# A planned kernel for a gated recurrence and a two-layer block: new load costs in the planner, weight reloads in fewer transfers, and another order of the last products and stores

## The chip, the cores and the metric

The kernel runs on one core of one Trainium2 chip. The metric is device time in microseconds (us), from one launch of the kernel. The kernel before was run ten times: median 593.34 us, lowest 590.56, highest 594.98. One more execution was recorded by the hardware profiler; it took 590.61 us, of which 588.9 lie between its first and last instruction. Its mean granted TensorE clock was 0.995 of full speed.

## The reference

Everything is computed in 32-bit floats. A gated recurrence comes first (batch 4, 8 heads, 768 tokens, 48 dims a head), then a block of two matrix products with `h - tanh(h)` between them:

```python
state = np.zeros((B, H, D, D), dtype=np.float32)
for t in range(S):
    state = alpha[:, :, t, :, None] * state + np.einsum('bhd,bhe->bhde', k[:, :, t], v[:, :, t])
    y[:, :, t] = np.einsum('bhd,bhde->bhe', q[:, :, t], state)

x = y.transpose(0, 2, 1, 3).reshape(B * S, H * D)     # 3072 tokens x 384
h = x @ w_in                                          # 384 x 2048
g = h - np.tanh(h)
out = g @ w_out                                       # 2048 x 384
```

The two weights reach the kernel as 64-bit words, and the kernel turns them into 32-bit floats itself.

## The kernel before

**Units.** The 3072 tokens are cut into 12 units of 256 tokens, three to a batch, and a unit into two chunks of 128. Names of tasks carry their unit: `scores 5.0` is chunk 0 of unit 5, `first 3:7` is step 7 of unit 3.

**The recurrence, for each unit.** SP loads alpha, k, q and v (`load aT`, `load kT`, `load qT`, `load v`, in the function `load`; alpha, k and q are four transfers each, v is six from unit 2 on, where `halved` is true, and two before). ScalarE spreads each of the first three in its raw buffer (`wide aT`, `wide kT`, `wide qT`, L639), and VectorE transposes them in blocks (`aT`, `kT`, `qT`, L647: the "flip"; four instructions each). Two scans on VectorE make products of alpha along the tokens (`U`, L719, and `W`, L738); k and q are multiplied with them (`kU`, `qW`). For a chunk TensorE then does `scores` (L816 from unit 2 on), VectorE masks them (`masked`, L838), TensorE does `y`, with the update of the state in it (L866, L878, L917), and `back`, a transpose of k (L904), whose result ScalarE copies out as `natural` (L908). ScalarE also copies y out as `x`, and SP shifts some rows of it into place by six small transfers (`moves`, L960). `sizeU` and `sizeW` are ScalarE's checks of the scans' magnitude.

**The two products, for each unit.** They run in eight steps. `first u:s` makes a 256-wide piece of h (L1026: six products; each product of 32-bit floats is two records in the trace, so 12), ScalarE squares it (`square`, L1035, and `quad`, L1039), VectorE makes `cube` (L1043) and `shrunk` (L1047), which is g. `large` (L1053) is a check of magnitude on every second step. Units 0 and 1 are "plain": `second` is then four matrix products of 384 columns (L1071) into two accumulators. From unit 2 on, `sums` (L1059, L1060) builds five sums of blocks of g, and `second` (L1086) is seven products of 192 columns instead of eight, in the manner of Strassen, into four accumulators `o0` to `o3` with two halves each (14 records). The weights' side of these sums is built once by `combine 0` to `combine 4` on VectorE. `store u` puts the accumulators together: ScalarE copies o2 as `p` (L1124), four VectorE operations make `same` and `cross` from it, o1, o3 and o0 (L1127), and four transfers store them, two of `cross` (L1134) and two of `same` (L1137). For the last unit the two of `cross` are issued by ScalarE's queue, all others by SP.

**The weights.** Sixteen pieces, a w_in piece and a w_out piece for each step, go through raw buffers, four at a time: `fetch` (SP, L43), `read` (ScalarE, L86 and L87), and the conversion on VectorE (L89 and L90), a task that is named after its piece (`in5`, `out2`). The text calls a landed piece by the same name. The pieces are planned in the order in0, in1, in2, in3, out0, in4, out1, in5, out2, in6, out3, in7, out4 to out7. Later, when TensorE runs at full rate, each piece is read once more for a check of its range: `reload n` (SP) and `look n` (ScalarE, L104 and L105), with a single raw buffer, so that `reload n` waits for `look n - 1`. A w_in piece is eight transfers (its padded rows are split, the wide ones tile by tile), a w_out piece is one (`weight_parts`).

**The order.** No engine's order is written by hand. Each piece of work is a task with a name, an engine, a reckoned duration, a rank, the tasks it comes after, and a latency until its followers may start; `add(name, engine, us, rank, after, do, lat)`. The `Planner` simulates the engines eight times over, with priorities worked out from the end backwards and some seeded noise in the later rounds, keeps the shortest plan, and the instructions are issued in the order of the plan's start times. So each engine runs its tasks strictly in that order, and a different duration of any one task can reorder all engines. `filler` puts small products (L1148) into the plan's gaps of TensorE before `y 0.0`.

**The end.** `judge` (VectorE), `gather` (TensorE) and `ok` (VectorE) reduce all the checks to one integer. SP loads it into a register (`values_load`, L1222), and a branch leads to a slower general version (`general`, L1223) if a check failed. It isn't taken here.

The lines that the change touches, but for the functions printed below, are these:

```python
566  add(f"fetch {what}{s}", "SP", 4.1 if what == "in" else 2.0, ..., lat=2.5)
628  go(f"load {name}", "SP", 1.3 if direct or ... else 2.0, ..., lat=2.5)
962  go("moves", "SP", 2.5, 17, ..., moves, lat=2.5)
1005 add(f"reload {n}", "SP", 1.0, ..., lat=6.0)
1104 add(f"second {me}", "PE", 2.65 if plain else 2.29, ...)
```

(The first of them is not touched; it stands for comparison.)

Of the kernel before, what the change touches and what calls it, by code (L numbers as in the profile page):

```python
# [19 lines left out]
CU = 2  # L20
# [25 lines left out]

def weight_parts(w_in, w_out, pad_rows, what, s):

    if what == "out":
        return [(slice(0, P), slice(0, 2), w_out.rearrange("(j p) n -> p j n", p=P)[:, 2 * s:2 * s + 2, :])]  # L50
    parts = []
    for i in range(len(pad_rows[0])):
        at, f0 = pad_rows[0][i]
        step = pad_rows[1][i][1] - f0
        src = w_in[f0:f0 + len(pad_rows) * step].rearrange("(j p) n -> p j n", p=step)
        src = src[0:at.stop - at.start, :, 2 * s * P:2 * (s + 1) * P]

        few = at.stop - at.start < 32
        parts += [(0, at, slice(0, len(pad_rows)), src)] if few else [(j - 9, at, slice(j, j + 1), src[:, j:j + 1]) for j in range(len(pad_rows))]
    return [x[1:] for x in sorted(parts, key=lambda x: (x[0], x[1].start))]  # L60
# [364 lines left out]
def fast(tc, q, k, v, alpha, moe_w_in, moe_w_out, out, w_in, w_out, ident, ok, pad_rows):  # L425
    nc = tc.nc
# [6 lines left out]
    NU = B * UPB  # L433
# [4 lines left out]
    PLAIN = 2  # L438
# [4 lines left out]
    with ExitStack() as ctx:  # L443
# [23 lines left out]
        def halved(u):  # L467


            return u >= len(TURNED)  # L470

        def by_matmul(u, what):
            return u < len(TURNED) and what in TURNED[u]
# [135 lines left out]
        def gla(u, rank):  # L609
# [12 lines left out]
            def go(name, engine, us, k, after, do, of=u, **kw):  # L622
                add(f"{name} {of}", engine, us, rank + k,
                    [a if a[-1] in "0123456789" else f"{a} {of}" for a in after if a], do, **kw)

            prev = f" {u - 1}" if u > 0 else None
            for what, name in enumerate(("aT", "kT", "qT", "v")):
                go(f"load {name}", "SP", 1.3 if direct or u == 1 and by_matmul(u, what) else 2.0, -9 + 0.1 * what,
                   [what < 3 and u > 0 and not by_matmul(u - 1, what) and not by_matmul(u, what) and f"{name}{prev}"]
                   + [u == 1 and ("kUba 0" if what == 3 else "turn qTb 0")]  # L630
                   + [f"{last} {u - 2}.{CU - 1}" for last in ("y", "state") if what == 3 and u > 1
                      and (last == "y" or (u - 2) % UPB < UPB - 1)],
                   lambda what=what: load(u, what), lat=2.5)

# [326 lines left out]
            if not direct:  # L961
                go("moves", "SP", 2.5, 17, [f"x {u}.{CU - 1}"], moves, lat=2.5)

# [33 lines left out]
        def reload(n):  # L997
            looked[n] = load_weight(nc, combo_pool[0], weight_parts(moe_w_in, moe_w_out, pad_rows, *pieces[n]))

# [3 lines left out]
        for n in range(len(pieces)):  # L1003
            rank = 2 * FS * 3 + 8 * n
            add(f"reload {n}", "SP", 1.0, rank, ["combine 4", n > 0 and f"look {n - 1}"], lambda n=n: reload(n), lat=6.0)
            add(f"look {n}", "ACT", 2.2, rank + 4, [f"reload {n}"], lambda n=n: look(n))
# [3 lines left out]
        def moe(u, rank, gait):  # L1010
# [3 lines left out]
            def step(s):  # L1014
# [48 lines left out]
                def second():  # L1063
# [12 lines left out]
                    e, o = m["e", s], m["o"]  # L1076
                    w = w_out[:, 2 * s:2 * s + 2, :].rearrange("p a (b n) -> p a b n", b=2)

                    for n, i, g_, w_ in ((2, 1, e[:, 1, :], w[:, 0, 0]),
                                         (1, 0, g[:, 1, 1, :], combos["21-11"][:, s]),  # L1080
                                         (1, 1, g[:, 0, 0, :], combos["12-22"][:, s]),
                                         (2, 0, e[:, 0, :], w[:, 1, 1]),
                                         (3, 0, e[:, 3, :], combos["-21-22"][:, s]),
                                         (3, 1, e[:, 2, :], combos["11+12"][:, s]),
                                         (0, 0, e[:, 4, :], combos["11+22"][:, s])):
                        T.matmul(o[n][:, i], lhsT=g_, rhs=w_, start=(s == 0 and (n, i) in ((0, 0), (1, 0), (2, 1), (3, 0))),  # L1086
                                 stop=(s == FS - 1), skip_group_check=True)

# [13 lines left out]
                if not plain:  # L1102
                    add(f"sums {me}", "DVE", 1.2, r + 1.1, [f"shrunk {me}"], sums)
                add(f"second {me}", "PE", 2.65 if plain else 2.29, r + 5,
                    [f"out{s}" if plain else "combine 4", f"sums {me}" if not plain else f"shrunk {me}"]
# [8 lines left out]
            def store():  # L1114
# [17 lines left out]
                for c in range(CU):  # L1132
                    half = [out_r[u * CU + c][:, n * NH:(n + 1) * NH] for n in range(2)]
                    (A if u == NU - 1 else nc.sync).dma_start(out=half[1 - c], in_=cross[:, c, :])  # L1134
                for c in range(CU):
                    half = [out_r[u * CU + c][:, n * NH:(n + 1) * NH] for n in range(2)]
                    nc.sync.dma_start(out=half[c], in_=same[:, c, :])  # L1137
            add(f"store {u}", "DVE", 2.6 if not plain else 0.1, rank + gait * FS + 4.9, [f"second {u}:{FS - 1}"], store,
# [115 lines left out]
```

## Time and profile before

| what | value |
|---|---|
| median of ten runs | 593.34 us (590.56 to 594.98) |
| the profiled execution | 590.61 us |
| its span, first to last instruction | 588.9 us |
| granted TensorE clock | 0.995 |
| last matrix product ends | 581.03 us |
| weight transfers SP issues for w_in, fetched and reloaded | 128, of 96 KB each, 3.1 us to landing |
| the same for w_out | 16, of 768 KB each, 5.0 us to landing |

The profile is of one execution. Its page gives, for each engine, its busy time and its share of the span, then groups of instructions by line and shape with their number and mean duration, and for each the idle time ahead of it and what ended that idle time. The trace behind the page lists each instruction with its start in us, its duration, its engine and line, and in brackets how long the engine had been idle before it and what released it. The chain of waits is the list of such rows followed back from a chosen instruction, in order of time. PE is TensorE, PEld its loading of weights, DVE VectorE, ACT ScalarE, SP the engine that issues most transfers.

### The profile page before, as it was taken

The numbers are of one execution on the slowest core, as the hardware profiler recorded it, in microseconds if no ns is written. First come the engines' busy times: TensorE is split into PE (matmuls) and PEld (weight loads), VectorE is DVE, ScalarE is ACT, GpSimd is POOL, SyncE is SP. The second block draws the span as 40 slices with busy tenths as digits, with TensorE's granted clock in tenths as the row PEclk, the third lists the DMA queues.
The fourth block names the chain that finished last, engine by engine and source line by source line (L and its number), as shares of the span: only waits on it lengthen the run. The fifth ranks groups of instructions, "written<-read, shape, count | busy, mean of one in ns | idle before, by whom it ended". The sixth has DMA issues, their size and how long they took to land.

```text
span 588.9 us, 11492 instructions
## 1 busy us (share of the span) xinstructions
PE 573.6 (97%) x4425; PEld 504.5 (86%) x4425; DVE 443.7 (75%) x868; ACT 322.1 (55%) x565; POOL 5.8 (1%) x22
## 2 busy tenths in 40 slices
PE   8899999999999999999999999999999999999994
PEld 7777777769988979999998999898899898899994
DVE  6888898988969968886886787877698735634642
ACT  3788995548567676495485364265343423423530
POOL 3000000000000000000000000000000000000000
PEclk9999999999999999999999999999999999999998
DMA  8899952043463533443352120220010000000001
GB/s 186 201 251 245 272 123 75 28 102 94 104 173 117 144 98 112 103 140 111 88 153 63 29 62 28 51 64 28 28 35 1 28 8 2 28 8 0 28 1 35
DMA packets 61856, 50.70 MB, mean 86 GB/s; under 512 B 36928, under 2 KB 51552, under 8 KB 61792
## 3 DMA queue, kind: packets, MB, share of 16 engines
q1 hardware_dynamic: 58880, 48.89, 31.3%
q10 hardware_dynamic: 2912, 0.98, 0.8%
q8 instruction: 37, 0.61, 0.5%
q14 instruction: 27, 0.22, 0.1%
HBM read 44.04 MB, written 4.72 MB: 83 GB/s over the span
## 4 chain that ended last, share of the span: by engine, by line
PE 82%; DMA 5%; DVE 4%; ACT 4%; SPq 2%; issue 2%; POOL 0%; ACTq 0%; DVEq 0%; POOLq 0%
PE h L1026 37%; PE o L1086 27%; PE o L1071 7%; PE sc L878 3%; PE sc L816 3%; DMA raw<-in_moe_w_in_dram 2%; PE sc L866 2%; DMA ar<-in_alpha_dram 1%; PE sc L917 1%; DVE U L719 1%; PE sc L904 1%; PE spin L1148 1%; ACT u L1035 1%; SPq L43 1%; ACT junk L752 1%
## 5 line engine op out<-in xcount | busy, mean ns | idle before, releaser
L1026 PE MATMUL h<-xT,w_in 128*128 128x256 f32 x1152 | 265.7, 380 | 1.4 <-DVE w L1043 1.0
L1026 PEld LDWEIGHTS h<-xT,w_in 128*128 128x128 f32 x1152 | 215.0, 190 | 30.3 <-DVE w_in L90 1.2
L1035 ACT ACTIVATE u<-h 128x512 f32<-128x512 f32 x96 | 57.0, 594 | 166.8 <-PE h L1026 166.4
L1043 DVE TENSOR_TENSOR w<-h,u 128x512 f32<-128x512 f32 x96 | 66.1, 689 | 90.9 <-ACT u L1035 90.3
L1086 PE MATMUL o<-b,e 128*128 128x192 f32 x480 | 91.1, 326 | 0.0
L1086 PE MATMUL o<-w_out,e 128*128 128x192 f32 x320 | 81.3, 336 | 0.0
L1086 PEld LDWEIGHTS o<-b,e 128*128 128x128 f32 x480 | 80.2, 190 | 0.0
L1047 DVE SCALAR_TENSOR_TENSOR g<-z,w 128x512 f32<-128x512 f32 x96 | 66.0, 687 | 10.3 <-ACT z L1039 5.5
L1086 PE MATMUL o<-b,g 128*128 128x192 f32 x320 | 65.1, 326 | 0.0
L1039 ACT ACTIVATE z<-u 128x512 f32<-128x512 f32 x96 | 60.3, 628 | 2.3
L1086 PEld LDWEIGHTS o<-w_out,e 128*128 128x128 f32 x320 | 56.0, 190 | 4.7 <-issue 0.5
L1086 PEld LDWEIGHTS o<-b,g 128*128 128x128 f32 x320 | 54.2, 190 | 0.0
L1053 ACT ACTIVATE big<-u 128x1024 f32<-128x1024 f32 x48 | 50.2, 1047 | 0.0
L1071 PE MATMUL o<-w_out,g 128*128 128x384 f32 x128 | 44.2, 489 | 0.0
L1071 PEld LDWEIGHTS o<-w_out,g 128*128 128x128 f32 x128 | 23.9, 190 | 13.6 <-DVE w L1043 0.2
L1059 DVE TENSOR_TENSOR e<-g 128x256 f32<-128x256 f32 x80 | 33.3, 416 | 1.6
L1060 DVE TENSOR_TENSOR e<-g 128x256 f32<-128x256 f32 x80 | 33.4, 418 | 0.0
L838 DVE TENSOR_TENSOR pm<-sc,mask 64x256 f32<-64x256 f32 (+1 forms) x60 | 28.7, 506 | 2.7 <-PE sc L816 2.4
L738 DVE TENSOR_TENSOR_SCAN W<-aT,before 128x1032 f32<-128x1032 f32 (+1 forms) x13 | 27.7, 2134 | 0.0
L719 DVE TENSOR_TENSOR_SCAN U<-aT,after 128x1032 f32<-128x1032 f32 (+1 forms) x13 | 27.6, 2133 | 0.1
L639 ACT COPY ar<-ar 32x512 f32<-32x512 f32 x22 | 13.6, 616 | 21.0 <-DMA ar<-in_alpha_dram 13.2
L816 PEld LDWEIGHTS sc<-qT,kT 48*64 48x64 f32 x640 | 15.2, 133 | 9.2 <-issue 4.3
(125 smaller groups left out, 551.8 us busy)
## 6 DMA issues: line engine op xcount, KB each, us to landing
raw<-in_moe_w_in_dram SPq DMA_DIRECT2D x128, 96.0 KB, 3.1
raw<-in_moe_w_out_dram SPq DMA_DIRECT2D x16, 768.0 KB, 5.0
ar<-in_alpha_dram SPq DMA_DIRECT2D x44, 96.0 KB, 2.2
kr<-in_k_dram SPq DMA_DIRECT2D x40, 96.0 KB, 2.3
qr<-in_q_dram SPq DMA_DIRECT2D x40, 96.0 KB, 2.2
vt<-in_v_dram SPq DMA_DIRECT2D x20, 96.0 KB, 2.5
vt<-in_v_dram SPq DMA_DIRECT2D x40, 48.0 KB, 2.4
out_dram<-same SPq DMA_DIRECT2D x20, 96.0 KB, 1.7
```

The source lines that it names most:

```text
L719: V.tensor_tensor_scan(out=m["U"][:, ns].rearrange("p n t -> p (n t)")[:, ::-1], data0=aT[:, z:a:-1], data1=after[:, a:z][:, ::-1], initia ...
L816: T.matmul(sc[r][rows:rows + HP, g, HP * half:], lhsT=m["kT"][q, g, c, rows:rows + HP], rhs=m["qT"][q, g, c, HP * half:], start=True, stop ...
L1026: T.matmul(h[:, a, :], lhsT=w_in[:, j, f * P:(f + 1) * P], rhs=xT[u][:, j, :], start=(j == 0), stop=(j == KT - 1))
L1035: A.activation(m["u", s], m["h", s], AF.Square, scale=W_SCALE ** -1.5)
L1039: A.activation(m["z", s], m["u", s], AF.Square, bias=QB, scale=QA * W_SCALE)
L1043: V.tensor_mul(m["w", s], m["h", s], m["u", s])
L1047: V.scalar_tensor_tensor(out=g.rearrange("p a c t -> p (a c t)"), in0=m["z", s], scalar=QK, in1=m["w", s], op0=ALU.add, op1=ALU.mult)
L1053: A.activation(big, m["us", s // 2].rearrange("p s t -> p (s t)"), AF.Relu, bias=-U_FAST, scale=W_SCALE, accum_out=over[:, n:n + 1])
L1059: V.tensor_add(e[:, 0:2, :], g[:, 0], g[:, 1])
L1060: V.tensor_sub(e[:, 2:4, :], g[:, :, 1, :], g[:, :, 0, :])
L1071: T.matmul(m["o"][c], lhsT=g[:, a, c, :], rhs=w_out[:, f, :], start=(f == 0), stop=(f == FT - 1))
L1086: T.matmul(o[n][:, i], lhsT=g_, rhs=w_, start=(s == 0 and (n, i) in ((0, 0), (1, 0), (2, 1), (3, 0))), stop=(s == FS - 1), skip_group_chec ...
```

## The change

It has four parts.

1. Durations that the planner reckons for SP's tasks: loads from unit 2 on (and those of unit 1 that are not transposed by TensorE) 2.2 instead of 2.0, `load v` 3.9 where it is six transfers, `moves` 3.9 instead of 2.5, a reload 2.0 for a w_in piece and 0.5 for a w_out piece instead of 1.0. The latency behind a load from unit 2 on is 4.5 instead of 2.5. These are numbers of the plan alone; the plan, and with it each engine's order, comes out different.
2. A reload of a w_in piece is four transfers instead of eight: `weight_parts` gets a parameter that keeps the tiles of a row group together.
3. In the last unit, step 6 does four of its seven products, and the other three are done in step 7, whose order is: its own first four, then the older two into o3, its own two into o3, the older one into o0, its own into o0. The planner's durations of the two tasks become 1.3 and 3.28.
4. Of the last four stores, the two of chunk 0 (one `cross`, one `same`) are issued by ScalarE's queue and the two of chunk 1 by SP.

```diff
--- before.py
+++ after.py
@@ -44,7 +44,7 @@
     return raw
 
 
-def weight_parts(w_in, w_out, pad_rows, what, s):
+def weight_parts(w_in, w_out, pad_rows, what, s, by_tile=True):
 
     if what == "out":
         return [(slice(0, P), slice(0, 2), w_out.rearrange("(j p) n -> p j n", p=P)[:, 2 * s:2 * s + 2, :])]
@@ -55,7 +55,7 @@
         src = w_in[f0:f0 + len(pad_rows) * step].rearrange("(j p) n -> p j n", p=step)
         src = src[0:at.stop - at.start, :, 2 * s * P:2 * (s + 1) * P]
 
-        few = at.stop - at.start < 32
+        few = at.stop - at.start < 32 or not by_tile
         parts += [(0, at, slice(0, len(pad_rows)), src)] if few else [(j - 9, at, slice(j, j + 1), src[:, j:j + 1]) for j in range(len(pad_rows))]
     return [x[1:] for x in sorted(parts, key=lambda x: (x[0], x[1].start))]
 
@@ -625,12 +625,12 @@
 
             prev = f" {u - 1}" if u > 0 else None
             for what, name in enumerate(("aT", "kT", "qT", "v")):
-                go(f"load {name}", "SP", 1.3 if direct or u == 1 and by_matmul(u, what) else 2.0, -9 + 0.1 * what,
+                go(f"load {name}", "SP", 1.3 if direct or u == 1 and by_matmul(u, what) else 3.9 if what == 3 and halved(u) else 2.2, -9 + 0.1 * what,
                    [what < 3 and u > 0 and not by_matmul(u - 1, what) and not by_matmul(u, what) and f"{name}{prev}"]
                    + [u == 1 and ("kUba 0" if what == 3 else "turn qTb 0")]
                    + [f"{last} {u - 2}.{CU - 1}" for last in ("y", "state") if what == 3 and u > 1
                       and (last == "y" or (u - 2) % UPB < UPB - 1)],
-                   lambda what=what: load(u, what), lat=2.5)
+                   lambda what=what: load(u, what), lat=2.5 if u < PLAIN else 4.5)
 
             def widen(what):
                 for hh in range(2):
@@ -959,7 +959,7 @@
                         r0 = HP * hh + f0 - (H - 2 + hh) * D
                         nc.sync.dma_start(out=xT[u][part, j, :], in_=xT[u][r0:r0 + part.stop - part.start, KT, :])
             if not direct:
-                go("moves", "SP", 2.5, 17, [f"x {u}.{CU - 1}"], moves, lat=2.5)
+                go("moves", "SP", 3.9, 17, [f"x {u}.{CU - 1}"], moves, lat=2.5)
 
 
 
@@ -995,14 +995,14 @@
         looked = {}
 
         def reload(n):
-            looked[n] = load_weight(nc, combo_pool[0], weight_parts(moe_w_in, moe_w_out, pad_rows, *pieces[n]))
+            looked[n] = load_weight(nc, combo_pool[0], weight_parts(moe_w_in, moe_w_out, pad_rows, *pieces[n], by_tile=False))
 
         def look(n):
             junk = two.tile([P, N * (P + 1)], FP32, name="junk", bufs=1)
             too_wide(nc, junk, looked.pop(n), most[:, n:n + 1], tiny[:, n:n + 1])
         for n in range(len(pieces)):
             rank = 2 * FS * 3 + 8 * n
-            add(f"reload {n}", "SP", 1.0, rank, ["combine 4", n > 0 and f"look {n - 1}"], lambda n=n: reload(n), lat=6.0)
+            add(f"reload {n}", "SP", 2.0 if pieces[n][0] == "in" else 0.5, rank, ["combine 4", n > 0 and f"look {n - 1}"], lambda n=n: reload(n), lat=6.0)
             add(f"look {n}", "ACT", 2.2, rank + 4, [f"reload {n}"], lambda n=n: look(n))
 
         steps = []
@@ -1075,16 +1075,22 @@
                         m["o"] = [ps_o.tile([P, 2, NH], FP32, name=f"o{n}") for n in range(2 * CU)]
                     e, o = m["e", s], m["o"]
                     w = w_out[:, 2 * s:2 * s + 2, :].rearrange("p a (b n) -> p a b n", b=2)
-
-                    for n, i, g_, w_ in ((2, 1, e[:, 1, :], w[:, 0, 0]),
-                                         (1, 0, g[:, 1, 1, :], combos["21-11"][:, s]),
-                                         (1, 1, g[:, 0, 0, :], combos["12-22"][:, s]),
-                                         (2, 0, e[:, 0, :], w[:, 1, 1]),
-                                         (3, 0, e[:, 3, :], combos["-21-22"][:, s]),
-                                         (3, 1, e[:, 2, :], combos["11+12"][:, s]),
-                                         (0, 0, e[:, 4, :], combos["11+22"][:, s])):
-                        T.matmul(o[n][:, i], lhsT=g_, rhs=w_, start=(s == 0 and (n, i) in ((0, 0), (1, 0), (2, 1), (3, 0))),
-                                 stop=(s == FS - 1), skip_group_check=True)
+                    now = [(s, *x) for x in ((2, 1, e[:, 1, :], w[:, 0, 0]),
+                                             (1, 0, g[:, 1, 1, :], combos["21-11"][:, s]),
+                                             (1, 1, g[:, 0, 0, :], combos["12-22"][:, s]),
+                                             (2, 0, e[:, 0, :], w[:, 1, 1]),
+                                             (3, 0, e[:, 3, :], combos["-21-22"][:, s]),
+                                             (3, 1, e[:, 2, :], combos["11+12"][:, s]),
+                                             (0, 0, e[:, 4, :], combos["11+22"][:, s]))]
+
+                    if u == NU - 1 and s == FS - 2:
+                        now, m["rest"] = now[:4], now[4:]
+                    elif u == NU - 1 and s == FS - 1:
+                        now = now[:4] + m["rest"][:2] + now[4:6] + m["rest"][2:] + now[6:]
+
+                    for s_, n, i, g_, w_ in now:
+                        T.matmul(o[n][:, i], lhsT=g_, rhs=w_, start=(s_ == 0 and (n, i) in ((0, 0), (1, 0), (2, 1), (3, 0))),
+                                 stop=(s_ == FS - 1), skip_group_check=True)
 
                 add(f"first {me}", "PE", 2.62, r,
                     [f"in{s}" if plain else None, f"cube {older[2]}" if older[2] else f"masked 0.{CU - 1}"]
@@ -1101,7 +1107,7 @@
                     add(f"large {me}", "ACT", 1.2, r + 2, [f"square {me}"], large)
                 if not plain:
                     add(f"sums {me}", "DVE", 1.2, r + 1.1, [f"shrunk {me}"], sums)
-                add(f"second {me}", "PE", 2.65 if plain else 2.29, r + 5,
+                add(f"second {me}", "PE", 2.65 if plain else 1.3 if me == f"{NU - 1}:{FS - 2}" else 3.28 if me == f"{NU - 1}:{FS - 1}" else 2.29, r + 5,
                     [f"out{s}" if plain else "combine 4", f"sums {me}" if not plain else f"shrunk {me}"]
                     + ([f"store {n}" for n in range(max(0, u - 2 if u <= PLAIN else u - 1), u)] if s == 0 and u >= PLAIN else [])
                     + ([f"state {PLAIN - 1}.{c}" for c in range(CU) if (PLAIN - 1) % UPB * CU + c < NCH - 1]
@@ -1131,10 +1137,10 @@
                 put(same, o[0][:, 0:1, :].to_broadcast([P, 2, NH]), ALU.add, same)
                 for c in range(CU):
                     half = [out_r[u * CU + c][:, n * NH:(n + 1) * NH] for n in range(2)]
-                    (A if u == NU - 1 else nc.sync).dma_start(out=half[1 - c], in_=cross[:, c, :])
+                    (A if u == NU - 1 and c == 0 else nc.sync).dma_start(out=half[1 - c], in_=cross[:, c, :])
                 for c in range(CU):
                     half = [out_r[u * CU + c][:, n * NH:(n + 1) * NH] for n in range(2)]
-                    nc.sync.dma_start(out=half[c], in_=same[:, c, :])
+                    (A if u == NU - 1 and c == 0 else nc.sync).dma_start(out=half[c], in_=same[:, c, :])
             add(f"store {u}", "DVE", 2.6 if not plain else 0.1, rank + gait * FS + 4.9, [f"second {u}:{FS - 1}"], store,
                 lat=1.0)
             yield
```

## The prediction

> **What bounds the kernel now.** I read the page's head first, then TensorE in order of time, then the chain of waits around each hole, then the last 10 us.
>
> ```profile
> span 588.9 us, 11492 instructions
> PE 573.6 (97%) x4425; PEld 504.5 (86%) x4425; DVE 443.7 (75%) x868; ACT 322.1 (55%) x565; POOL 5.8 (1%) x22
> ```
>
> TensorE is busy 97% of the span, and nothing in the diff removes a multiplication. So the time can only change in three places: the start until TensorE is saturated, holes after that, and what follows the last matmul. Steady rates: a `first` (12 records) takes 2.59 us from its start to the next task's, a `second` (14 records) 2.27, a plain `second` (8) 2.58. Comparing each task with these, TensorE is back to back from 50.5 us to the end but for three holes, at the first row of the task behind each:
>
> ```profile
> 174.98 0.67 PE L866 MATMUL sc<-qT,state 48*64 48x128 f32 x16 [0.46 <-DVE pm L838]
> ...
> 214.60 0.90 PE L816 MATMUL sc<-qT,kT 48*64 48x128 f32 x32 [1.41 <-ACT kn L908]
> ...
> 398.05 0.90 PE L816 MATMUL sc<-qT,kT 48*64 48x128 f32 x32 [0.48 <-ACT kn L908]
> ```
>
> The tasks before them began at 172.09, 210.42 and 394.80. They took 2.89, 4.18 and 3.25 where 2.27, 2.59 and 2.59 are due: holes of 0.62, 1.59 and 0.66, **2.87 us** together. The chain of waits of the second shows the cause of all three:
>
> ```profile
> 203.93 5.59 DMA ar<-in_alpha_dram
> ...
> 209.60 0.63 ACT ar L639
> ...
> 210.24 1.02 ACT junk L104 x2
> ...
> 214.01 0.54 ACT kn L908
> ```
>
> ScalarE takes its work in a fixed order. It stands at `wide aT 7` (L639), which waits for alpha, and `square 3:6` and `natural 5.0`, which TensorE needs, stand behind it. Alpha is late because SP issues about one small transfer in 0.46 us: v takes 3.87 us (197.92 to 201.79), the moves 3.68, alpha and k 2 each. Before hole one, SP issued 32 transfers in a row (151.22 to 169.08), 8 of them a reload; ScalarE then waited 3.75 us at `wide aT 6`. The planner reckoned v at 2.0, moves at 2.5, a reload at 1.0.
>
> **Middle: costs in the planner, fewer reload transfers.** The four w_in reloads that count (0 to 3) and four later ones fall from 8 transfers to 4. Eight are 8 x 0.46 = 3.7 us of SP (161.69 to 165.32), four about 1.85, so alpha behind one comes 1.8 us earlier. [...] The merged transfer itself, 48 partitions by 3 pieces, is not in the trace: between 2.5 us (landing of a 96 KB piece) and 6.0 (768 KB of w_out), I take 4; `look` comes over 7 us after its reload, so it hides both ends. SP's order stays nearly the same; its queue is moved past little (moves 2 and 3 now ahead of v).
>
> More is in the orders. In the changed program `wide aT 6` stands behind `square`, `quad` and `large` of 2:7, not ahead; `wide aT 7` behind `quad 3:6`, `look 6` and `natural 5.0`; `wide aT 11` (hole three) behind `square`, `sizeU`, `quad` and `large` of 7:5. For the third nothing moves on SP: v waits for `y 8.1` at 377.5, then 3.9 + 3.9 + 2.2, landing 389.9; but the squares no longer wait behind it. I cost the holes at **-2.87** (ends -3.2 and 0). What is late next: `natural 5.0` behind `look 6`. The reload lands near 207, look ends near 212, `scores 5.0` wants it near 214, 1.5 us spare. If that cover goes, each us is paid.
>
> **Start.** Weight transfers keep DMA busy 0.9 to 1.0 of the time from 20 to 60 us, so landings, not issues, set the pace. A `first` waits for every w_in conversion placed before it in the plan, even a later step's: `first 0:3` restarted at the end of the conversion for step 4 (45.07 + 0.96).
>
> ```profile
> 46.08 2.43 PE L1026 MATMUL h<-xT,w_in 128*128 128x256 f32 x10 [0.25 <-DVE w_in L90]
> ...
> 50.49 0.62 ACT L639 COPY ar<-ar 32x512 f32<-32x512 f32 x1 [1.34 <-DMA ar<-in_alpha_dram]
> ...
> 52.57 1.08 ACT L86 ACTIVATE more<-raw 128x768 int16<-128x768 uint32 x1
> ```
>
> Before, in5 was converted (done 50.39) before out2, and `first 0:4` ran at 50.5. Now VectorE has out2 ahead of in5, and ScalarE has `read out2` ahead of `square 0:3`. Out2 landed at 49.78 (issued 43.78, 6.0 us). Fetch in5 may go out 1.8 us sooner, as it takes another buffer, but it queues behind the same data, and so does out2: same landing. Then: read out2 49.8 to 51.8; out2's L90 0.96 to 52.8; in5's two operations 0.55 + 0.96 to 54.35. TensorE does `second 0:1` in the meantime and is ready for `first 0:4` at about 51.7 (first 0:2 and 0:3 come earlier by 0.6 and 1.4, which is thrown away here). It does its first matmul, waits to 54.35 and ends at 56.7. Before, the same two tasks were done at 55.78: **+0.9 us**. Ends: -1.0 (out2 lands 2 us sooner) and +2.7 (it takes 7.8, the longest landing of these transfers up to 75 us).
>
> Load aT 2 (1.87 us of SP at 45.06) goes behind out4, so in6 lands near 53 rather than 55.4, and later pieces follow. Its flip (4 transposes, 2.07) moves on VectorE from 51.9 into this stretch:
>
> ```profile
> 70.00:80.00 10.00, 10.00 (x40) 7.41 (x39) 9.58 (x15) 9.11 (x15) 0.00 (x0) 1.00 0.70 161
> 80.00:90.00 10.00, 10.00 (x40) 6.82 (x39) 9.97 (x18) 9.48 (x17) 0.00 (x0) 1.00 0.55 124
> ```
>
> (Columns: window, length, busy PE, PEld, DVE, ACT.) VectorE is 98% full there. Walking the new list from 54.35, `shrunk 0:7` ends at 76.0, W 2 at 87.3, qW 2 at 91.5, and `scores 2.0` wants qW 2 at 95.6. The thinnest cover is about 1 us at `first 0:7` (in7 converted once `first 0:6` ends, cube 0:5 behind it) and 1.5 at `second 0:4`. So zero; without cover 2.07. The other moves at the start (v 1 ahead of out0, sizeW 1 and wide aT 1 later) delay out0 by about 2 us; its conversion still waits for ScalarE and VectorE, not for the landing: zero.
>
> **End.**
>
> ```profile
> 580.09 0.49 ACT L1124 ACTIVATE p<-o 128x384 f32<-128x384 f32 x1 [5.93 <-PE o L1086]
> ...
> 581.56 1.21 DVE L1127 SCALAR_TENSOR_TENSOR same<-o,same 128x384 f32<-128x384 f32 x2
> 581.67 0.88 ACTq L1134 DMA_DIRECT2D out_dram<-cross  x2
> 582.79 0.84 SPq L1137 DMA_DIRECT2D out_dram<-same  x2
> ```
>
> Step 6 gives three of its seven products to step 7, behind step 7's first four. The last matmul stays at 581.03, but o2 and o1 are complete 3 x 0.325 = 0.98 us sooner, so p starts at 579.11. The four VectorE operations follow at the same distances: the last at 581.23, just after the last matmul, ends at 581.8 instead of 582.77. `gather` and the step's sums (done 576.3) are in time. Of the last two stores SP now issues one: 0.43 saved (a cross store goes to SP, long before). [...] The trace: SP's load of `ok` starts at 583.69, right behind its second issue, then a branch until 586.97, then its closing waits to 588.1; the last landing is at 586.82 and none waits for it. So both count: 0.98 + 0.43 = **-1.4 us** (ends -1.5 and -0.5, as branches now meet closer together).
>
> **Sum.** +0.9 - 2.87 - 1.4 = -3.4 us. Against the profiled execution: span 588.9 to 585.5, 590.61 to 587.2. That execution lies at the low end of the runs (median 593.34); taken off the median: **589.9 us**, -0.57%. About 0.3%, 1.8 us, can be told from no change.
>
> **Rivals.** (1) The holes only move: TensorE's feeders are reordered in each unit, and new holes of the size of the old open elsewhere. For it: ScalarE 90 to 98% busy in stretches such as 210 to 220. Against: ends of waits had several us of cover in the walk through units 2 to 7. +0.9 - 1.4 - some 0.5 = 592.3. Chance 0.22. (2) Out2 lands early, or in5 is not held: start -0.7 instead of +0.9: 588.3. Chance 0.13. (3) Slower: weights arrive too late for an order that puts w_out ahead of w_in. Place: out2 before in5, out3 before in7, out4 before cube 0:6, on ScalarE and VectorE. Price: out2 at its longest landing +1.8, each further pair the 2.0 us of a read that stands in ScalarE's way: 0.9 + 1.8 + 4.0 - 4.3 = +2.4, 595.7. It decides once landings are 1 to 1.5 us later than I walked, the cover above. For it: DMA is saturated there. Against: aT 2's move frees it. Chance 0.15. My forecast: 0.50, own range 588.4 to 591.4.
>
> **Numbers.** Range: the forecast's, (2), (1) and nearly nothing of (3): 587.5 to 593.8. Faster: 0.47 of the forecast, (2), a little of (1): 0.63. Same: the rest of both: 0.22. Slower: 0.15.
>
> **What would show it.** Right: a hole of 2.6 us in `first 0:4` with the release by the w_in conversion; the start of `second 0:2` near 56.7; no wait for L908 of over 0.3 us at TensorE from 160 to 400; `p` 1 us earlier against the last matmul, SP issuing one `same` store. Wrong: holes past 60 us with waits for L90 (rival 3), or new ones behind looks (rival 1).

## The result, and the profile after

The changed kernel takes 589.45 us (median of 15 runs, 587.56 to 591.09), the kernel before 593.30 (52 runs). The ratio is 0.9933, 95% interval 0.9918 to 0.9948: faster by 0.67%. Its profiled execution took 587.96 us; its page begins

```profile
span 586.2 us, 11454 instructions
PE 573.4 (98%) x4425; PEld 504.4 (86%) x4425; DVE 444.5 (76%) x868; ACT 323.0 (55%) x565; POOL 5.8 (1%) x22
```

The multiplications are the same (573.4 us of 573.6), so 2.7 us of span came out of places where TensorE stood. The three places of the forecast, each read by its own view:

**Middle.** What TensorE waited for between 160 and 410 us (columns: who waited, for whom, us in all, times, longest). First the kernel before, then the changed one, where the list is empty:

```profile
engine line waited for: us in total, times, longest us
PE sc L816 <- ACT kn L908: 1.9, 2, 1.4
PE sc L866 <- DVE pm L838: 0.5, 1, 0.5
```

```profile
core 0 of [0], span 586.2 us
engine line waited for: us in total, times, longest us
```

Task for task, TensorE makes up 0.53 us at `second 2:6`, 1.48 at `first 3:7` and 0.55 at `first 7:7`, 2.55 together, and loses none of it again.

**Start.** The changed kernel's rows in order of time (start, duration, engine, line, operation; in brackets the idle time and what ended it):

```profile
49.65 1.07 ACT L86 ACTIVATE more<-raw 128x768 int16<-128x768 uint32 x1 [1.61 <-DMA raw<-in_moe_w_out_dram]
...
51.66 0.96 DVE L90 CUSTOM_DVE_ANT_0 w_out<-bits,more 128x1536 uint16<-128x1536 uint16 x1 [1.48 <-ACT more L87]
...
52.25 0.59 PE L1026 MATMUL h<-xT,w_in 128*128 128x256 f32 x2
...
53.23 0.96 DVE L90 CUSTOM_DVE_ANT_0 w_in<-bits,more 128x1536 uint16<-128x1536 uint16 x1
...
54.24 2.43 PE L1026 MATMUL h<-xT,w_in 128*128 128x256 f32 x10 [1.40 <-DVE w_in L90]
...
56.51 2.74 PE L1071 MATMUL o<-w_out,g 128*128 128x384 f32 x8
```

This is the walk of the forecast: out2 lands (49.56), is read and converted, and only then comes in5, and `first 0:4` has done one of its six products and stands. `second 0:2` starts at 56.51 (forecast: near 56.7). The hole is shorter than forecast, because TensorE comes to `first 0:4` at 52.25, not near 51.7: from there to the release it is 1.99 us (forecast: 2.6), of which TensorE stands 1.40. From `first 0:6` on, TensorE is 0.73 us later than before (61.68 against 60.95).

**End.** The changed kernel's last rows, and what SP waited for there:

```profile
577.29 0.49 ACT L1130 ACTIVATE p<-o 128x384 f32<-128x384 f32 x1 [4.96 <-PE o L1092]
...
578.75 1.21 DVE L1133 SCALAR_TENSOR_TENSOR same<-o,same 128x384 f32<-128x384 f32 x2
...
579.99 0.33 SPq L1143 DMA_DIRECT2D out_dram<-same  x1
580.00 0.37 ACTq L1143 DMA_DIRECT2D out_dram<-same  x1
```

```profile
SPq L1228 <- SPq L1228: 3.3, 1, 3.3
```

The last product ends at 579.21 (before: 581.03), so `p` starts 1.92 us ahead of it instead of 0.94, and the last VectorE operation ends 0.76 us behind it instead of 1.73: 0.98 gained, as forecast. But SP's wait on its own branch line, 2.6 us before (the row `SPq L1222 <- SPq L1222: 2.6, 1, 2.6`), is 3.3 now. From the last product to the end of the span it is 7.02 us; it was 7.85. So the end gains 0.83.

The account of the two traces: +0.73 - 2.55 - 0.83 = -2.65 us, which is the difference of the profiled times (590.61 - 587.96).

### The profile page after: what moved, and what is told of

The parts are those of the page before. It is cut to its first block, busy times and chain, and to the rows that moved or that the text cites. A ratio compares the mean times of both kernels' runs of the same rounds, so it can differ in the third digit from the quotient of the medians.

```text
span 586.2 us, 11454 instructions
## 1 busy us (share of the span) xinstructions
PE 573.4 (98%) x4425; PEld 504.4 (86%) x4425; DVE 444.5 (76%) x868; ACT 323.0 (55%) x565; POOL 5.8 (1%) x22
## 4 chain that ended last, share of the span: by engine, by line
PE 91%; DMA 4%; DVE 2%; ACT 1%; issue 1%; SPq 0%; POOL 0%; DVEq 0%; ACTq 0%; POOLq 0%
PE h L1026 41%; PE o L1092 32%; PE o L1071 6%; PE sc L878 3%; PE sc L816 3%; DMA raw<-in_moe_w_out_dram 2%; PE sc L866 2%; PE sc L917 1%; PE sc L904 1%; DMA raw<-in_moe_w_in_dram 1%; DMA rough<-in_k_dram 1%; PE spin L1154 1%; DVE W L738 0%; PE turned L671 0%; DVE w_in L90 0%
## 5 line engine op out<-in xcount | busy, mean ns | idle before, releaser
L1061 DVE TENSOR_TENSOR e<-g 128x128 f32<-128x128 f32 x80 | 22.7, 284 | 0.0
L894 ACT COPY xT<-sc 112x512 f32<-112x512 f32 x20 | 11.7, 584 | 19.7 <-PE sc L917 9.7
```

## The experiments

Eleven kernels. Executions differ in the first 50 us (the next run and the kernel before by 3.7 us) and by the clock (last section), so a single span says little, and the three runs on the end alone have one timed execution each; effects below 1 us are read from the trace, as the step in TensorE's lead or lag from one task to the next.

### Only the order of the last products

The kernel before, with the changed kernel's list of products in `second` (its core below) and the planner's durations left alone:

```diff
+                    if u == NU - 1 and s == FS - 2:
+                        now, m["rest"] = now[:4], now[4:]
+                    elif u == NU - 1 and s == FS - 1:
+                        now = now[:4] + m["rest"][:2] + now[4:6] + m["rest"][2:] + now[6:]
```

> The kernel before, with nothing but the other order of the last products (its planner and so all orders elsewhere are the old ones). Theory: TensorE's last product stays at 581.0 us, p and the four VectorE operations come 0.98 us earlier against it, SP still issues two stores of same; all engines' branches move by the same 0.98, so SP's branch keeps its 2.67 us and the span falls by 0.98, to 587.9. Rival: nothing of the earlier sums reaches the end, because the branch or the landing of the last store sets it: span 588.5 or more.

The span was 590.8; `first 0:0` started 3.7 us later than in the kernel before (31.65 against 27.93), behind a stretch of half clock (last section). Behind the last product: the last VectorE operation ends at +0.76 us instead of +1.73, and the span ends at +7.25. The tail, from the last product to the end of the span, is 7.85, 7.93, 7.96 and 8.27 us long in the runs with the old end, so some 0.6 to 1.0 of the 0.98 arrives. SP's branch stays short, as expected:

```profile
SPq L1229 <- SPq L1229: 2.8, 1, 2.8
```

### Only the split of the last stores

```diff
-                    (A if u == NU - 1 else nc.sync).dma_start(out=half[1 - c], in_=cross[:, c, :])
+                    (A if u == NU - 1 and c == 0 else nc.sync).dma_start(out=half[1 - c], in_=cross[:, c, :])
-                    nc.sync.dma_start(out=half[c], in_=same[:, c, :])
+                    (A if u == NU - 1 and c == 0 else nc.sync).dma_start(out=half[c], in_=same[:, c, :])
```

> The kernel before, with nothing but the last four stores dealt out anew (one cross and one same each on ScalarE's queue and on SP). Theory of the forecast: SP issues one store fewer, 0.43 us, and the span falls by that, to 588.5. Rival, from the changed kernel's trace, where three engines branch within 0.7 us of each other and SP's branch takes 3.33 us instead of 2.67: SP comes to its branch 0.4 us earlier and leaves it at the same time or later: span 588.8 to 589.1, the split is worth nothing.

The tail is 7.94 us: nothing gained that shows. SP reaches its branch 0.52 us sooner (2.75 us behind the last product instead of 3.27) and leaves it at 6.03 instead of 5.94, with ScalarE and VectorE branching within 0.8 us of it:

```profile
SPq L1222 <- SPq L1222: 3.2, 1, 3.2
```

### Both changes at the end

The two edits above together in the kernel before.

> The kernel before, with both changes at the end (order of the last products, stores dealt out anew) and nothing else. Forecast: 1.4 us off the span, to 587.5. By the changed kernel's trace: the last product to the end of the span is 7.0 us there and was 7.9, so 0.9 us, to 588.0. If the split is worth nothing, this equals the run with the order of products alone.

Tail 7.19 us; the kernels of this study with the changed end have 7.02 to 7.32. That is the run with the order of products alone (7.25) within their spread. The split adds nothing that can be seen in it; the forecast 0.43 us would have given 6.8.

### Only the reloads in fewer transfers

The kernel before, all orders as they were (`weight_parts` gets the parameter of the changed kernel as well):

```diff
-            looked[n] = load_weight(nc, combo_pool[0], weight_parts(moe_w_in, moe_w_out, pad_rows, *pieces[n]))
+            looked[n] = load_weight(nc, combo_pool[0], weight_parts(moe_w_in, moe_w_out, pad_rows, *pieces[n], by_tile=False))
```

> The kernel before, with nothing but w_in reloads of four transfers instead of eight; planner and orders are the old ones. Theory: SP comes to alpha of units 6 and 7 about 1.8 us sooner, so the holes at second 2:6 (0.62 us) and first 3:7 (1.59) close or nearly, the third, at first 7:7, stays, as no w_in reload that is issued next to it delays its alpha: span 588.9 - 2.1 = 586.8. Rival (the orders closed the holes, the reloads are hidden anyway): all three holes stay, span 588.5 or more.

The rival won. The time is 593.89 us, ratio 1.0022 (0.9998 to 1.0045), and all three holes are there:

```profile
PE sc L816 <- ACT kn L908: 2.2, 2, 1.4
PE sc L866 <- DVE pm L838: 0.8, 1, 0.8
```

Hole one is 0.35 us larger, hole three 0.27, and 0.19 are new at `scores 6.0`. Of these only hole one has a merged reload just ahead of its alpha, and it stands out: in the four other traces with the old orders and eight transfers (the three runs above and the kernel before) it stays within 0.14 us, while hole three is anything between nothing and 0.32 us more than in the kernel before. The 0.19 are in none of the four, but alpha lands there as before; their cause stays open. At hole two there was nothing to save: the reload just ahead of that alpha is one of w_out, a single transfer in both. Around `wide aT 6` the trace of the kernel before reads

```profile
161.69 3.63 SPq L43 DMA_DIRECT2D raw<-in_moe_w_in_dram  x8
...
165.42 1.78 SPq L606 DMA_DIRECT2D ar<-in_alpha_dram  x4
...
168.85 0.62 ACT L639 COPY ar<-ar 32x512 f32<-32x512 f32 x1 [3.75 <-DMA ar<-in_alpha_dram]
```

and with the merged reload, in a trace where all is about 2.4 us later here (`qr` is issued at 162.06 instead of 159.66):

```profile
164.09 1.80 SPq L43 DMA_DIRECT2D raw<-in_moe_w_in_dram  x4
...
165.99 1.78 SPq L606 DMA_DIRECT2D ar<-in_alpha_dram  x4
...
171.72 0.62 ACT L639 COPY ar<-ar 32x512 f32<-32x512 f32 x1 [4.18 <-DMA ar<-in_alpha_dram]
```

SP does issue alpha 1.83 us sooner, to the digit of the forecast: 1.90 us from the start of the reload instead of 3.73. But ScalarE waits longer. The view of the tile `ar` in this stretch says why, first before, then merged:

```profile
DMA to landing us min/median/max: 2.8/2.9/2.9
```

```profile
DMA to landing us min/median/max: 5.1/5.2/5.3
```

The bytes of the reload are the same, and alpha, issued sooner, takes 2.3 us longer. In both kernels its first transfer lands 0.4 us behind the reload's last (168.32 against 167.90 before, 171.28 against 170.87 merged), and the reload itself needs 6.8 us from its first issue to its last landing in four transfers, 6.2 in eight. So alpha came when the reload's data was through, and SP's issuing was hidden behind that.

### The changed kernel with reloads of eight transfers

The reverse edit of this line, in the changed kernel, with its durations kept.

> The changed kernel, but w_in reloads are eight transfers again; its planner's durations and all its orders stay. Theory of the forecast (transfers count where the next load waits for SP): alpha of units 6 and 7 comes up to 1.8 us later and holes of 0.5 to 1.5 us open again at TensorE between 160 and 220 us: span 587.0 to 588.5. Rival (the orders alone close the holes, since spreading alpha now stands behind the squares): no hole, span 586.2 within 0.2.

Again the rival: from 160 to 410 us TensorE waits for nothing,

```profile
core 0 of [0], span 590.2 us
engine line waited for: us in total, times, longest us
```

and no task from `second 0:2` to the end is more than 0.06 us off the changed kernel's pace. The time, 590.54 us, ratio 0.9945 (0.9918 to 0.9971), can't be told from the changed kernel's. The reload's transfers are worth nothing in the new orders; the new orders are the gain of the middle.

### Three waits moved by hand in the old orders

The kernel before, where the planner's finished list is edited before it is issued:

```diff
+        for x, y in (("wide aT 6", "large 2:7"), ("wide kT 6", "wide aT 6"), ("wide aT 7", "natural 5.0"), ("wide kT 7", "wide aT 7"), ("wide aT 11", "large 7:5")):
+            name = [self.tasks[t[3]][0] if t[3] is not None else None for t in filled]
+            t = filled.pop(name.index(x)); name.remove(x); filled.insert(name.index(y) + 1, t)
         return filled
```

> The kernel before, with five tasks of ScalarE moved and nothing else: wide aT 6 and wide kT 6 behind large 2:7, wide aT 7 and wide kT 7 behind natural 5.0, wide aT 11 behind large 7:5. Reloads, planner and stores are the old ones. Theory (the holes come from where ScalarE stands and waits for alpha, not from how long SP takes for a reload): against the kernel before, TensorE gains 0.53 at second 2:7, 1.48 at scores 5.0 to second 3:5 and 0.55 at scores 9.0, 2.5 us in all, with nothing lost elsewhere; time 0.4% less. Rival (the changed kernel needed the rest of its new orders or its reloads too): at most half of this, or new holes at U 6, U 7 or U 11 behind the later spreads.

The three gains come to the digit: 0.53, 1.48, 0.55 us. But 1.18 us are lost between them, at a place where the kernel before had no hole. Ratio 0.9945 (0.9920 to 0.9969), by which alone it couldn't be told from the next run.

```profile
252.35 0.62 ACT L642 COPY ar<-ar 32x512 f32<-32x512 f32 x1 [5.51 <-DMA ar<-in_alpha_dram]
...
260.82 0.51 ACT L911 COPY kn<-sc 128x448 f32<-128x448 f32 x1
...
261.38 0.90 PE L819 MATMUL sc<-qT,kT 48*64 48x128 f32 x32 [1.11 <-ACT kn L911]
```

TensorE is now 2 us further when alpha of unit 8 lands, and the same pattern repeats one unit on: ScalarE at `wide aT 8` for 5.5 us, `natural 6.0` behind it and behind 8.5 us of other work that ScalarE does from then on without a break. Two more moves of the same kind were tried:

```diff
+        ... ("wide aT 8", "natural 6.0"), ("wide kT 8", "wide aT 8")
```

> The kernel before, with the five moves of the wide-only run and two more of the same kind: wide aT 8 and wide kT 8 behind natural 6.0. Theory (the hole of 1.1 us that opened at scores 6.0 when the earlier ones closed is the same wait of ScalarE for alpha, one unit on): it closes, and TensorE gains 2.55 us in all against the kernel before, as the changed kernel did from 160 us on. Rival: the hole moves on again, to unit 7 or later, or DVE is late with U 8.

The hole closes, and no other opens: 2.56 us gained over the kernel before, what the changed kernel gains in this stretch (2.55), with nothing of the change but the place of seven tasks on ScalarE.

```profile
core 0 of [0], span 589.6 us
engine line waited for: us in total, times, longest us
```

The time is 589.30 us, ratio 0.9942 (0.9925 to 0.9959).

### The start: in5 ahead of out2

The changed kernel with the task in5 moved ahead of out2 on VectorE:

```diff
-        return filled
+        at = {self.tasks[x[3]][0]: n for n, x in enumerate(filled) if x[3] is not None}; filled.insert(at["out2"], filled.pop(at["in5"])); return filled
```

> The changed kernel, with one thing moved: VectorE converts in5 ahead of out2, as the kernel before did; all else stays. Theory: in5 is converted near 50.7 us, the hole of 1.67 us in first 0:4 goes, out2 is converted by 52.7 as before and second 0:2 follows at 54.84; at most 0.3 is given back at first 0:5, which waits for in6: TensorE is 1.4 us earlier from first 0:6 on, span 584.8. Rival (weights' landings and ScalarE's reads set the pace there, and the hole only moves to first 0:5 or second 0:3): span 585.8 to 586.4.

`second 0:2` came 1.62 us earlier, and 1.39 of it was given back in the next task, `first 0:5` (587.55 us, ratio 0.9918, 0.9887 to 0.9949). The rival's place, but by another cause than landings alone:

```profile
51.52 1.07 ACT L86 ACTIVATE more<-raw 128x768 int16<-128x768 uint32 x1 [2.43 <-DMA raw<-in_moe_w_out_dram]
...
57.93 0.96 DVE L90 CUSTOM_DVE_ANT_0 w_in<-bits,more 128x1536 uint16<-128x1536 uint16 x1 [1.51 <-ACT more L87]
...
58.95 5.02 PE L1026 MATMUL h<-xT,w_in 128*128 128x256 f32 x22 [1.12 <-DVE w_in L90]
```

ScalarE stood 2.43 us at the read of out2 (landed 51.44 here), did `square 0:3`, `x 1.1`, `quad 0:3` and `large 0:3` after it, and so read in6, which had landed at 53.94, only from 55.92. `first 0:5` waited for in6. The fault of the new start is on both engines. So the second half was mended as well, again by moving tasks in the changed kernel's list:

```diff
+        for x, y in (("in5", "shrunk 0:2"), ("read out2", "quad 0:3"), ("out2", "read out2"), ("large 0:3", "square 0:4")):
+        ... (each x moved behind its y, as in the run with three waits moved)
```

> The changed kernel, with the start mended on two engines: VectorE converts in5 ahead of out2, and ScalarE does square 0:3, x 1.1 and quad 0:3 ahead of reading out2, and large 0:3 behind square 0:4, so that the read of in6 comes earlier. Theory (in the run with in5 first, ScalarE stood 2.4 us at the read of out2 with 3.4 us of ready work behind it, and that made in6 late for first 0:5): the hole of 1.4 to 1.7 us is gone from first 0:4, first 0:5 and first 0:6, and TensorE is 1.5 us ahead of the changed kernel from first 0:6 on, 0.8 ahead of the kernel before. Rival (landings of the weights set the pace): the hole turns up again before second 0:4, net gain under 0.4 us.

```profile
52.49 2.75 PE L1029 MATMUL h<-xT,w_in 128*128 128x256 f32 x12
...
55.08 2.74 PE L1074 MATMUL o<-w_out,g 128*128 128x384 f32 x8
...
57.66 5.34 PE L1029 MATMUL h<-xT,w_in 128*128 128x256 f32 x24
```

No wait in any of them, although out2 landed late again (51.52). TensorE is 1.67 us ahead of the changed kernel's pace from here to its last product. 586.66 us, ratio 0.9899 (0.9874 to 0.9924); the span of the traced execution is 584.9 against 586.2.

### Who issues the last stores

In the changed kernel, for the last unit:

```diff
+                if u == NU - 1:
+                    for t, first, step in ((cross, NH, -NH), (same, 0, NH)):
+                        to = bass.AP(tensor=out_r[u * CU].tensor, offset=out_r[u * CU].offset + first, ap=[[d_model, P], [P * d_model + step, CU], [1, NH]])
+                        A.dma_start(out=to, in_=t)
+                    return
```

> The changed kernel, but the last unit's stores are two transfers instead of four, one of cross and one of same for both chunks, both issued by ScalarE's queue, none by SP. Theory (the end is set by the last engine's branch and by SP's closing waits after its own, 1.1 us; not by issues): SP branches before the last sums and has its closing waits done when the last landing comes; ScalarE leaves its branch 5.0 us after the last product, so from the last product to the end 5.8 to 6.2 us instead of 7.0 to 7.3. Rival (the end waits for the landing of the last store, and one transfer of twice the size lands later): 7.0 us or more.

Inconclusive as to its theory. The two hand-written store patterns span overlapping stretches of memory, so `same` was made to wait for the landing of `cross`: ScalarE sat 2.19 us and issued it 2.33 us behind the last product instead of 0.79. Even so the tail was 6.77 us (587.97 us, ratio 0.9916, 0.9887 to 0.9945). A version without that wait, on top of the mended start:

```diff
-                    (A if u == NU - 1 and c == 0 else nc.sync).dma_start(out=half[1 - c], in_=cross[:, c, :])
+                    nc.sync.dma_start(out=half[1 - c], in_=cross[:, c, :])
-                    (A if u == NU - 1 and c == 0 else nc.sync).dma_start(out=half[c], in_=same[:, c, :])
+                    (A if u == NU - 1 else nc.sync).dma_start(out=half[c], in_=same[:, c, :])
```

> The changed kernel with the mended start, and the last stores dealt out in a third way: both of cross by SP, both of same by ScalarE's queue. Theory: SP issues its last at 0.1 us after the last product, branches at 1.1 and is through its closing waits (1.1 us) when ScalarE, which branches at 2.3 us, comes out at 5.3; from the last product to the end 6.2 to 6.4 us (changed kernel and its variants: 7.0 to 7.3). With the start's 1.6 us: span 584.1, time 0.4% below the changed kernel, 0.985 to 0.99 of the kernel before. Rival (the landing of the last store sets the end): 7.0 us or more, span 584.9.

The tail is 6.44 us, at the edge of what the theory gave: SP leaves its branch 4.06 us behind the last product instead of 5.11, and its closing waits end on the last landing (4.78). So the rival has a share too: landing and branch now end within 0.4 us of each other. 586.75 us, ratio 0.9903 (0.9878 to 0.9928). The medians of this run and of the one with the mended start alone (0.9899) lie below both kernels of the case; all four executions of the latter are faster than the changed kernel's fastest (587.56). From each other the two can't be told by the time. The traced execution of this one had the slow start of the last section (span 587.2); the four of its six timed executions with a clock of 0.996 or more span 584.4 to 585.4.

## Why the prediction was right, and where it was not

The forecast was 589.9 us, measured 589.45. The sum behind it was less good than this looks: -3.4 us against -2.65 in the two traces. That the median came out so near is in part luck, as the medians fell by 1.2 us more than the traces (below).

- **Start, +0.9.** Measured +0.73. The cause and the releaser were right, and the end of the hole (54.24, forecast 54.35) and the start of `second 0:2` came within 0.2 us of the walk; the hole itself was 0.6 us shorter, as TensorE came to it later. Also right: that the 0.6 us that `first 0:2` comes earlier is lost again, and that the later aT 2 costs nothing (no wait of TensorE from 60 to 80 us). Shown by the mended start, which takes back 1.67 us, more than the 0.73 lost: from `first 0:6` on it is 0.70 ahead of the kernel before.
- **Middle, -2.87.** The place, the cause (ScalarE standing at the spreading of alpha with TensorE's feeders behind it) and the new orders as the cure were right: the seven hand-moved tasks give 2.56, the unmerged changed kernel keeps all. The size was off by 0.3, and this is an error of the baseline: I took the shortest `second` (2.27) and `first` (2.59) as due, but the task just ahead of a `y` or a `scores` takes 0.1 us more by itself; in the changed kernel, without any hole, `second 2:6` takes 2.37 and `first 3:7` 2.70. The cover that was named for `scores 5.0` held: `look 6` ended at 211.30 (forecast near 212), and `scores 5.0` started at 213.32 without a wait.
- **The step that failed: "alpha behind one comes 1.8 us earlier".** SP issues it 1.83 us earlier and it lands later, as its own time to landing rises from 2.9 to 5.2 us. I let the row of SP's issues decide. Alone the edit even makes hole one larger, by 0.35 us, and in the new orders it is worth zero (no task is more than 0.06 us off). The row said how long SP was busy; it didn't say that the wait ended on SP. The view of alpha's time to landing, which was 4.4 to 5.6 us already at hole two, behind a 768 KB reload of w_out (alpha's last transfer issued 203.93, landed 209.52), could have told me.
- **End, -1.4.** The products' order gave its 0.98 at the last sum. The 0.43 for SP's issue was worth nothing, because I held SP's branch at its 2.67 us; the stated end of the range, "as branches now meet closer together", was the case. What ate the saving is the branch, not the transfer: in the changed kernel the last store had landed at 583.89, and SP came out of its branch at 584.32, 3.33 us after it had entered it.
- **Rivals.** That the holes only move (0.22) did happen, in the hand-moved kernel, at unit 8, by 1.1 us of 2.56; in the changed kernel it didn't. Rival 2, start -0.7, and rival 3, weights too late, did not occur; the start with w_out ahead of w_in cost 0.73 us, not the 6.7 that rival 3 came to.

The medians fell by 3.85 us, 1.2 more than the traces; the fastest executions, 590.56 and 587.56, are 3.0 apart. Where the rest of the 1.2 comes from stays open. The mean granted clock over all executions is 0.9933 before (68) and 0.9952 after (17), but this can't be turned into time, as it includes the end, where TensorE has nothing to do: the two traces differ by as much, 0.995 and 0.997, though neither has a dip before the last product. The clock is at half for the last 5.7 us of the one and the last 3.2 of the other. A candidate is the dip behind the hole at `scores 5.0` (last section): 1.68 us in two of five traces with that hole would be an estimated 0.7 us in the mean, and the new orders would remove its occasion with the hole. No run tests this.

## What to carry to other kernels

When one engine takes its work in a fixed order, look for the instruction that waits for a transfer with another engine's feeders behind it, and move it behind them: that alone was the gain of the middle here (2.56 us), and one has to walk on to the next unit, since closing a hole can uncover the same wait later (here 1.1 us at unit 8). An issuer that is busy is not yet the bound: before merging transfers, compare the issue times with the time to landing of the transfer that someone waits for (here it was issued 1.83 us sooner and took 2.3 us longer). A steady rate taken as a minimum over unlike neighbours overstates a hole (each of the three here by 0.1 us), and a saved issue ahead of a branch counts only if the branch doesn't take longer for it (here 0.52 us sooner into the branch and 0.09 us later out of it).

## What the runs showed of the hardware that was not expected

**The clock dips, and each dip comes with a stretch in which TensorE stood.** In seven of the thirteen traced executions it was lower in the first 45 us. Stretches (columns: window, length, busy PE, PEld, DVE, ACT and POOL, granted clock, DMA share, GB/s) of the run with the third split of the stores, where it is 0.77, and of the changed kernel:

```profile
14.75:29.50 14.75, 13.24 (x161) 10.97 (x162) 11.53 (x25) 8.14 (x16) 0.00 (x0) 0.77 0.97 207
```

```profile
14.75:29.50 14.75, 13.08 (x197) 10.85 (x196) 13.14 (x27) 9.85 (x19) 0.00 (x0) 1.00 0.87 204
```

TensorE is 3.7 us behind the changed kernel at `y 0.1` (27.97 us against 24.27), and 3.3 of it stay to the end of the start. In two runs the clock fell right behind the hole at `scores 5.0`, to 0.83 of a stretch of 10 us, and TensorE lost 1.68 us there. In a finer division of the same traces each of the nine dips ahead of the last product is a stretch at 0.50 that lasts 3.41 or 6.83 us:

| run | TensorE idle for, until | half clock from | for |
|---|---|---|---|
| only the order of the last products | 1.52, 17.30 us | 17.94 | 6.83 us |
| changed kernel, eight transfers | 1.51, 17.24 | 17.82 | 6.83 |
| three waits moved | 1.53, 17.22 | 17.76 | 6.83 |
| third split of the stores, start mended | 1.51, 17.21 | 17.79 | 6.83 |
| both changes at the end | 2.09, 37.70 | 37.74 | 3.41 |
| only the reloads | 2.14, 37.57 | 37.37 | 3.41 |
| two more waits moved | 3.24, 38.23 | 39.64 | 3.41 |
| only the split | 1.58, 215.26 | 216.51 | 3.41 |
| both changes at the end | 1.66, 217.44 | 218.65 | 3.41 |

An idle stretch alone doesn't do it: all thirteen traces have one of 1.5 us that ends between 15.9 and 17.3 us, and only the four in which it ended latest lose the clock there. The losses (1.68 and 3.7 us) are near half of the lengths in the table, an estimated 1.7 us for 3.41 us at half clock and 3.4 for 6.83. What sets off a dip wasn't tested. The dip behind `scores 5.0` was in two of the five traced executions with that hole and in none of the eight without, too few to call it a consequence.

**The branch at the end takes 2.6 to 4.6 us, and SP's was longer where engines branched together.** This is the branch that passes over the general version; the time is that from an engine's branch to its next instruction. SP's took 2.67 to 3.02 us where it branched over 1 us after the others, and 3.28 to 3.64 where VectorE, ScalarE and SP branched within 0.8 us. The shortest and the longest are ScalarE's and SP's in the run with two stores, where SP branched 2.4 us ahead of the last product. What an engine does in this time is not in the traces.
